# Turning the keys of a recurrent attention block: one whole-tile transpose and ScalarE copies in place of sixteen small transposes a unit

## The chip, the cores and the metric

The kernel runs on one core of a Trainium2 chip. A core has TensorE (PE, matmuls, with its weight loads shown apart as PEld), VectorE (DVE), ScalarE (ACT), GpSimd (POOL) and SyncE (SP, which issues transfers). Each engine works through its own instructions in the order in which they were written, and waits at semaphores for the others. The metric is the device time of one execution in microseconds; the median of three runs of the kernel before is 402.22 us.

## The reference

Two blocks follow each other. The first is a recurrent attention: with gates f = sigmoid(f_logit), a state of 48 x 48 for each of 4 batches and 8 heads is carried over 768 time steps.

```python
for t in range(S):
    state = f[:, :, t, :, None] * state + einsum('bhd,bhe->bhde', k[:, :, t], v[:, :, t])
    y[:, :, t] = einsum('bhd,bhde->bhe', q[:, :, t], state)
```

Its output, turned to 3072 tokens of 384 features, goes through the second block, a feed-forward layer with a maximum of three products:

```python
h = np.maximum(np.maximum(x @ w1, x @ w2), x @ w3)
return h @ w_out
```

## The kernel before, in words

**Units.** The attention is computed in 24 units (NU) of 64 time steps of two batches, so 128 tokens each. In a unit, features lie on the partitions: kh (the keys, scaled by the gates' products) and qh (the queries, scaled likewise) are 128 partitions by 512 elements: partition = one of two heads of a pair times 64 padded features; free = 4 head pairs, 2 batches, 64 tokens. The function scan (L342) makes running products of the gates on DVE; after turns the keys (L307, tile kt) and multiplies them to kh on POOL (L353); before does the same for the queries (L360, L307, L364).

**Keys by tokens.** The matmuls that add to the state (sums, L446) contract over tokens, so they need the keys with tokens on the partitions: ks, 128 tokens by 8 heads by 64. For units below 6 (BY_ROWS), PE turns them. For units 6 to 21, keys_by_blocks(u, n) does it for n = 0 to 3, one block of 32 tokens a call: four DVE transposes (L395) of 32 partitions by 128 elements, each of which turns 32 x 32 blocks of kh and writes them straight to the 32 partitions of the tokens.

**Order.** The order is written out by hand, and nothing reorders it. In a round of the loop over units u, with n = u + 1, five stretches of the second block's matmuls (fill) lie between the steps of the attention:

- a fill; keys_by_blocks(u, 2); values(u - 1), which writes the output bank y (L428) and ends with a 1x1 copy by ACT of one element of y (L435, tile seen); sums(u - 1) (L446); pairs(u) (L409, with the mask by DVE, L412); finish(u - 1), whose matmuls (L517) add to y and whose three ACT copies (L524) write xT; the new state (DVE, L461)
- loads; keys_by_blocks(u, 3); scan(n)
- a fill; after(n) and before(n); an ACT step of a check of the weights' range (L289)
- a fill; carry(n) (POOL, L370); a second ACT step of the check (L291)
- a fill; keys_by_blocks(n, 0)
- a fill; keys_by_blocks(n, 1); a third ACT step (L291); the sigmoids of unit u + 2 (ACT, L322, tile sig).

Between L435 and L517 there is a dependence: the last element that seen reads is one that L517 writes, so L517's first such matmul waits for ACT.

**The second block.** Groups of four units go through it with a lag of one group. Its matmuls are L555 and L802 for the first group and the preparation of the weights, L902 and L642 for the others. They write banks of PSUM that ACT and DVE read out in between: ACT by L910, L916, L925, L930, L937, L647, L698 and L727, DVE by L945, L952, L953 and L650. POOL makes sums of tiles (L606, L886) and adds (L920, L938). The order of their products and reads repeats with every four units from unit 9 on.

**Buffers.** The pool called work holds kh, ks and sig twice and kt (the turned keys of after) once.

Of the kernel before, what the change touches and what calls it, by code (L numbers as in the profile page):

```python
# [9 lines left out]
FP32 = mybir.dt.float32  # L10
# [36 lines left out]
C = 64  # L47
DP = 64
# [7 lines left out]
def kernel(  # L56
# [12 lines left out]
    nc = tc.nc  # L69
    B, H, S, D = q.shape  # L70
    HP = H // 2
    NU = B // 2 * (S // C)
    UT = 2 * C
# [16 lines left out]
    def fast():  # L90
        ctx = ExitStack()
        with ctx:
            work = ctx.enter_context(tc.tile_pool(name="work", bufs=2))
# [216 lines left out]
            ready = {}  # L310
# [74 lines left out]
            def keys_by_blocks(u, n):  # L385

                if BY_ROWS <= u < NU - 2:
                    kh = ready[u]["kh"]
                    if n == 0:
                        ready[u]["ks"] = work.tile([UT, H, DP], FP32, name="ks")  # L390
                    ks = ready[u]["ks"].rearrange("s (hp par) d -> s hp par d", par=2)
                    a, t0 = divmod(n * 32, C)
                    for p0 in range(0, 128, 32):
                        par, e0 = divmod(p0, DP)
                        nc.vector.transpose(ks[n * 32:(n + 1) * 32, :, par, e0:e0 + 32], kh[p0:p0 + 32, :, a, t0:t0 + 32])  # L395

            FOUR = [(par, a) for a in range(2) for par in range(2)]

# [620 lines left out]
            with tc.manual_schedule():  # L1019
# [123 lines left out]
                for step in HEAD.split():  # L1143
                    name = step.rstrip("0123456789")
# [4 lines left out]
                for u in range(GRP + 1, NU):  # L1149
                    n = u + 1  # L1150
                    part = EARLY if u < BY_ROWS else LATER if u < 2 * GRP else PART
                    if n == BY_ROWS:
                        scan(n)
                    fill(part)
                    keys_by_blocks(u, 2)
                    room_of_unit = room_of_pairs()
                    if u > GRP:
# [22 lines left out]
                    if u + 2 < NU:  # L1180
                        load_v(u + 2)
                    keys_by_blocks(u, 3)
                    if n < NU:
                        if n < BY_ROWS or n == BY_ROWS + 2:
# [26 lines left out]
                    if n == NU:  # L1211
                        finish(u, xT)
                        pack(3, 3, xT, both)
                        packed[u // GRP] = xT
                    keys_by_blocks(n, 0)
                    fill(part - 1000 if u < 2 * GRP else part)
                    keys_by_blocks(n, 1)
# [274 lines left out]
```

## Time and profile before

| | |
|---|---|
| median of three runs | 402.22 us (402.06 to 402.51) |
| span of the profiled execution, first to last instruction | 400.5 us |
| granted TensorE clock, mean | 0.998 |
| PE busy | 387.5 us |
| DVE busy | 297.6 us |
| POOL busy | 245.9 us |
| ACT busy | 179.8 us |

The profile is of one execution. The page gives the busy time of each engine, the span in slices, the chain of work that ended last, and the costliest groups of instructions by line. Other views show the instructions in order of time with the idle time of the engine before each and what released it, or sum up who waited for whom. L395 is line 395 of the kernel; an arrow such as ks<-kh names the tile written and the tile read. Times are in microseconds from the first instruction; the mean duration in a group is in nanoseconds.

### The profile page before, as it was taken

What the parts mean: (1) busy time and instruction counts of PE and PEld (TensorE: products, weight loads), DVE (VectorE), ACT (ScalarE), POOL (GpSimd) and SP (SyncE); (2) the same over time, 40 slices, a digit from 0 to 9 for tenths busy, and PEclk for the clock granted to TensorE, in tenths of its full rate; (3) what the DMA queues carried; (4) which work ended last, traced back from release to release, by engine and by line L of the source; (5) the groups of instructions that cost most, each with busy time, mean ns of one, the idle gap of its engine ahead of it and who ended that gap; (6) DMA issues with size and microseconds to landing.
All of it is one profiled execution on the core that took longest, in us unless ns stands there. A gap on an engine that the chain in (4) does not pass through costs nothing.

```text
span 400.5 us, 11665 instructions
## 1 busy us (share of the span) xinstructions
PE 387.5 (97%) x4654; PEld 338.4 (85%) x4654; DVE 297.6 (74%) x583; ACT 179.8 (45%) x430; POOL 245.9 (61%) x276
## 2 busy tenths in 40 slices
PE   5799999999999999999999999999999999999995
PEld 4678855569998889988899988899988899988995
DVE  7998998898989998987998997998985450012600
ACT  2588876413134523344532354434354335576110
POOL 2276655789997697287667377657577850525700
PEclk9999999999999999999999999999999999999999
DMA  8999877767564776776734577633672003541002
GB/s 166 249 286 303 227 194 119 151 99 124 104 92 89 117 132 151 124 121 87 153 90 84 75 117 94 172 53 72 85 160 82 1 19 102 133 142 61 2 20 64
DMA packets 181610, 47.21 MB, mean 118 GB/s; under 512 B 160496, under 2 KB 179248, under 8 KB 181552
## 3 DMA queue, kind: packets, MB, share of 16 engines
q1 hardware_dynamic: 177536, 45.52, 55.9%
q10 hardware_dynamic: 4016, 0.91, 1.1%
q8 instruction: 37, 0.61, 0.6%
q14 instruction: 21, 0.17, 0.1%
HBM read 37.75 MB, written 4.72 MB: 106 GB/s over the span
## 4 chain that ended last, share of the span: by engine, by line
PE 91%; DVE 4%; SPq 2%; issue 1%; DMA 1%; POOL 0%; DVEq 0%; POOLq 0%
PE p L902 20%; PE p L642 18%; PE tr L902 17%; PE tr L642 14%; PE p L555 6%; PE y L428 3%; PE p L802 3%; PE y L517 2%; PE a L409 2%; PE a L446 2%; SPq L187 2%; DVE r L342 1%; PE tr L302 1%; PE a L1086 1%; PE y L424 1%
## 5 line engine op out<-in xcount | busy, mean ns | idle before, releaser
L395 DVE STREAM_TRANSPOSE ks<-kh 32x128 f32<-32x128 f32 x256 | 77.4, 302 | 11.5 <-POOL kh L353 7.3
L902 PE MATMUL tr<-xT,placed 128*128 128x256 f32 x180 | 44.4, 384 | 0.0
L902 PEld LDWEIGHTS tr<-xT,placed 128*128 128x128 f32 x180 | 33.5, 190 | 4.9
L353 POOL TENSOR_TENSOR kh<-kt,r 128x512 f32<-128x512 f32 x18 | 31.9, 1772 | 8.5 <-DVE kt L307 8.5
L342 DVE TENSOR_TENSOR_SCAN r<-gate,from_one 128x520 f32<-128x520 f32 (+1 forms) x27 | 33.2, 1239 | 1.8 <-issue 1.2
L555 PE MATMUL p<-xT,w_in 128*128 128x256 f32 (+1 forms) x108 | 33.9, 456 | 0.0
L606 POOL TENSOR_TENSOR w_in<-hm 128x256 f32<-128x256 f32 x18 | 13.3, 738 | 32.5 <-DVE hm L953 29.8
L524 ACT COPY xT<-y 64x256 f32<-64x256 f32 (+1 forms) x60 | 22.1, 369 | 22.4 <-PE y L517 21.6
L269 POOL TENSOR_TENSOR w_in<-top_bits,rest_bits 128x384 uint32<-128x384 uint32 x18 | 21.0, 1170 | 16.4 <-DVE top_bits L262 12.2
L902 PE MATMUL tr<-xT,w_in 128*128 128x256 f32 x120 | 30.8, 379 | 0.0
L902 PE MATMUL p<-w_in,placed 128*128 128x256 f32 x120 | 30.4, 382 | 0.0
L650 DVE TENSOR_TENSOR o<-tr,w_in 128x384 f32<-128x384 f32 (+1 forms) x11 | 5.7, 521 | 33.0 <-PE tr L642 29.0
L642 PE MATMUL p<-placed,hm 128*128 128x192 f32 x144 | 29.7, 332 | 0.0
L902 PE MATMUL p<-xT,placed 128*128 128x256 f32 x120 | 29.2, 379 | 0.0
L642 PE MATMUL tr<-w_out,w_in 128*128 128x192 f32 x144 | 28.6, 326 | 0.0
L945 DVE TENSOR_TENSOR hm<-tr,hm 128x512 f32<-128x512 f32 x15 | 10.2, 683 | 22.8 <-PE tr L902 15.9
L352 POOL COPY ends<-r 128x8 f32<-128x8 f32 x18 | 5.7, 319 | 34.4 <-DVE r L342 34.4
L555 PEld LDWEIGHTS p<-xT,w_in 128*128 128x128 f32 x108 | 19.4, 190 | 8.4 <-issue 6.7
L902 PEld LDWEIGHTS p<-w_in,placed 128*128 128x128 f32 x120 | 22.4, 190 | 4.4 <-issue 1.5
L291 ACT ACTIVATE raw<-top_bits 128x384 f32<-128x384 f32 x48 | 25.2, 526 | 0.4
L902 PEld LDWEIGHTS tr<-xT,w_in 128*128 128x128 f32 x120 | 22.8, 190 | 3.1
L902 PEld LDWEIGHTS p<-xT,placed 128*128 128x128 f32 x120 | 22.7, 190 | 2.8
(183 smaller groups left out, 980.2 us busy)
## 6 DMA issues: line engine op xcount, KB each, us to landing
raw<-in_moe_w_dram SPq DMA_DIRECT2D x24, 384.0 KB, 4.4
v_ld<-in_v_dram SPq DMA_DIRECT2D x48, 96.0 KB, 3.5
placed<-in_moe_w_dram SPq DMA_DIRECT2D x12, 384.0 KB, 5.5
out_dram<-o SPq DMA_DIRECT2D x45, 96.0 KB, 2.2
placed<-in_moe_w_out_dram SPq DMA_DIRECT2D x6, 384.0 KB, 5.4
f_ld<-in_f_logit_dram SPq DMA_DIRECT2D x36, 64.0 KB, 2.9
k_ld<-in_k_dram SPq DMA_DIRECT2D x36, 64.0 KB, 2.6
q_ld<-in_q_dram SPq DMA_DIRECT2D x36, 64.0 KB, 2.5
```

What stands on the lines that cost most here:

```text
L269: nc.gpsimd.tensor_tensor(dst, by(top), by(rest), op=ALU.add)
L291: nc.scalar.activation(over, size, AF.Relu, scale=(-1 / HI_MIN, 1.0)[step - 1], bias=(1.0, -HI_END * (1 - 2.0 ** -24))[step - 1], accum_ou ...
L342: nc.vector.tensor_tensor_scan(r[:, x][:, ::-1], flat(gate)[:, x][:, ::-1], flat(from_one)[:, x][:, ::-1], 1.0, op0=ALU.mult, op1=ALU.max)
L353: (nc.vector if u < BY_ROWS else nc.gpsimd).tensor_tensor(kh.rearrange("p h a t -> p a h t"), kt, by_batch(r[:, 1:LEN + 1].rearrange("p (x ...
L395: nc.vector.transpose(ks[n * 32:(n + 1) * 32, :, par, e0:e0 + 32], kh[p0:p0 + 32, :, a, t0:t0 + 32])
L428: nc.tensor.matmul(y[o:o + DP, a, hp * C:(hp + 1) * C], lhsT=v_ld[s, 2 * hp + par, :], rhs=d["at"][s, par, hp, :], start=(hp == 0), stop=F ...
L524: nc.scalar.copy(xT[o, :, t0 + a * C:t0 + (a + 1) * C], y[i, a, 0:HP * C].rearrange("p (h t) -> p h t", h=HP))
L555: nc.tensor.matmul(p if w < TOK else p.rearrange("p (two t) -> p two t", two=2), lhsT=w_in[i][:, kt, j * 128:(j + 1) * 128], rhs=x[:, t.st ...
L606: engine.tensor_tensor(dst, x, y, op=op)
L642: nc.tensor.matmul(b[:, p * HD:(p + 1) * HD], lhsT=x, rhs=w, start=id(b) not in begun, stop=True, skip_group_check=True)
L802: nc.tensor.matmul(p[:, 0:DM], lhsT=w_in[0][:, a, j * 128:(j + 1) * 128], rhs=w_out[:, j, :], start=(j == 0), stop=(j == NJ - 1))
L902: nc.tensor.matmul(b[:, j * HALF:(j + 1) * HALF], lhsT=w[:, (2 * n + j) * 128:(2 * n + j + 1) * 128], rhs=x, start=begin and j == 0, stop= ...
```

## The change

At keys_by_blocks(u, 0), DVE now turns all of kh of the unit in one stream transpose, into a tile of 128 by 512 called turned. It takes its place in the single buffer of kt. A stream transpose turns each 32 x 32 block where it stands: the block of features e0 to e0 + 31 and tokens 32 n to 32 n + 31 ends up with its tokens on the partitions that the features had. In each of the four calls ACT then copies four such groups of blocks, 32 partitions by 4 x 32 elements, from the partitions p0 of their features to the partitions 32 n of their tokens in ks. Units below 6 and above 21 are as they were.

```diff
             def keys_by_blocks(u, n):
 
                 if BY_ROWS <= u < NU - 2:
-                    kh = ready[u]["kh"]
+                    d = ready[u]
                     if n == 0:
-                        ready[u]["ks"] = work.tile([UT, H, DP], FP32, name="ks")
-                    ks = ready[u]["ks"].rearrange("s (hp par) d -> s hp par d", par=2)
-                    a, t0 = divmod(n * 32, C)
+                        d["ks"] = work.tile([UT, H, DP], FP32, name="ks")
+                        d["turned"] = work.tile([128, 2 * HP, C], FP32, name="kt", bufs=1).rearrange(
+                            "p x t -> p (x t)").rearrange("p (h n d) -> p h n d", h=HP, d=32)
+                        nc.vector.transpose(d["turned"].rearrange("p h n d -> p h (n d)"),
+                                            d["kh"].rearrange("p h a t -> p h (a t)"))
+                    ks = d["ks"].rearrange("s (hp par) d -> s hp par d", par=2)
                     for p0 in range(0, 128, 32):
                         par, e0 = divmod(p0, DP)
-                        nc.vector.transpose(ks[n * 32:(n + 1) * 32, :, par, e0:e0 + 32], kh[p0:p0 + 32, :, a, t0:t0 + 32])
+                        nc.scalar.copy(ks[n * 32:(n + 1) * 32, :, par, e0:e0 + 32], d["turned"][p0:p0 + 32, :, n, :])
```

## The prediction

> **What bounds the kernel now.** First the page's busy times and the shares of its chain of waits, then busy time by stretch (columns: stretch, its length, busy time and instruction count of PE, PEld, DVE, ACT, POOL; granted clock, DMA share, GB/s).
>
> ```profile
> PE 387.5 (97%) x4654; PEld 338.4 (85%) x4654; DVE 297.6 (74%) x583; ACT 179.8 (45%) x430; POOL 245.9 (61%) x276
> PE 91%; DVE 4%; SPq 2%; issue 1%; DMA 1%; POOL 0%; DVEq 0%; POOLq 0%
> 240.00:270.00 30.00, 30.00 (x384) 26.78 (x383) 26.59 (x57) 12.57 (x30) 19.72 (x21) 1.00 0.57 106
> ```
>
> TensorE sets the end: in a stretch of the middle it is busy 30.00 of 30.00 us. DVE, busy 26.59 there, is nearly full but off the chain (4%). So no time is to be had by unloading DVE; the question is whether the added work on ACT stays hidden. ACT is busy only 12.57 of 30, but it serves its instructions in program order, and PE needs some of them at a fixed moment.
>
> **The prices.** The groups by line and form (count | busy us, mean ns | idle us before):
>
> ```profile
> L395 DVE STREAM_TRANSPOSE ks<-kh 32x128 f32<-32x128 f32 x256 | 77.4, 302 | 11.5 <-POOL kh L353 7.3
> L307 DVE STREAM_TRANSPOSE kt<-k_ld 128x512 f32<-128x512 f32 x18 | 12.3, 685 | 0.8 <-DMA q_ld<-in_q_dram 0.3 <-DMA f_ld<-in_f_logit_dram 0.3 <-DMA out_dram<-o 0.2
> L524 ACT COPY xT<-y 64x256 f32<-64x256 f32 x40 | 14.7, 367 | 0.6
> L245 ACT ACTIVATE top_bits<-top_bits 128x384 f32<-128x384 f32 x20 | 10.5, 524 | 0.6
> ```
>
> Removed: 256 DVE transposes of 302 ns, 16 for each of the units 6 to 21. Added on DVE: one whole-tile transpose a unit, priced like the keys' own, 0.69 us. DVE loses 77.4 - 16 x 0.69 = 66 us; worth nothing while PE is full. Added on ACT: 16 copies a unit of 32x128 floats. The trace has no ACT copy of this size from SBUF. Between L524's 367 ns for 256 elements and L698's 0.48 us for 384 (row below) ACT takes (480 - 367) / 128 = 0.88 ns an element. Going down from L245, which reads SBUF, 128 elements take 524 - 256 x 0.88 = 299 ns; going down from L524, which reads PSUM, 367 - 128 x 0.88 = 254 ns. The new copies read SBUF, so I take the first; three L524 copies in a row take 1.14 us (row below), some 0.02 each over their own time, hence 0.31 for a copy in a row of them, 1.24 for four, 79 us in all. Each group of four stands at the same four places of a unit, K0 to K3, where the four transposes stood.
>
> **Where they meet PE.** Each unit, ACT makes a 1x1 copy named seen (L435) of the output bank y; the matmuls of L517 write that place of y, so they cannot start before seen has read it, and PE's later matmuls queue behind them. K0 and K1 of unit n stand in the last part of the round before, K2 just ahead of the seen in unit n's own round. Timeline of unit 16 (start us, us, engine, line, tiles, count, idle before):
>
> ```profile
> 203.85 0.66 PE L409 MATMUL a<-qh,kh 48*64 48x64 f32 x32
> 204.07 1.25 DVE L395 STREAM_TRANSPOSE ks<-kh 32x128 f32<-32x128 f32 x4
> 205.34 0.69 DVE L412 TENSOR_TENSOR at<-a,mask 128x512 f32<-128x512 f32 x1
> 206.51 1.26 DVE L395 STREAM_TRANSPOSE ks<-kh 32x128 f32<-32x128 f32 x4
> ...
> 211.37 0.78 POOL L606 TENSOR_TENSOR w_in<-hm 128x256 f32<-128x256 f32 x1 [4.50 <-DVE hm L953]
> 212.12 0.48 ACT L647 COPY w_in<-p 128x384 f32<-128x384 f32 x1 [4.71 <-PE p L642]
> 215.37 0.48 ACT L698 COPY top_bits<-tr 128x384 f32<-128x384 f32 x1 [2.77 <-PE tr L642]
> 215.68 1.35 POOL L353 TENSOR_TENSOR kh<-kt,r 128x512 f32<-128x512 f32 x1
> 215.74 0.53 ACT L291 ACTIVATE raw<-top_bits 128x384 f32<-128x384 f32 x1
> 216.26 0.62 ACT L322 ACTIVATE sig<-f_ld 128x512 f32<-128x512 f32 x1
> 217.07 1.24 DVE L395 STREAM_TRANSPOSE ks<-kh 32x128 f32<-32x128 f32 x4 [1.07 <-POOL kh L353]
> 217.97 0.48 ACT L647 COPY w_in<-p 128x384 f32<-128x384 f32 x1 [1.09 <-PE p L642]
> 218.62 0.15 ACT L435 COPY seen<-y 1x1 f32<-1x1 f32 x1 [0.18 <-PE y L428]
> 219.31 0.63 PE L517 MATMUL y<-qh,state 48*48 48x64 f32 x32
> 220.00 1.14 ACT L524 COPY xT<-y 128x256 f32<-128x256 f32 x3 [1.23 <-PE y L517]
> ```
>
> Today DVE starts K0 at 217.07, as POOL's kh is ready only then; ACT has long gone on to L698 (215.37) and L291. In the changed kernel K0's copies stand on ACT between the first L647 and L698, and wait for the whole-tile transpose, which waits for kh. Behind that wait are queued L698, both steps of L291, sig, the second L647, K1, K2 and seen. Kh itself comes earlier: DVE drops the groups at 204.07 and 206.51. L412 still needs PE's pairs (end 204.51), so it gains 0.8 instead of 1.25, and with 1.26 the chain over DVE hm L953 to POOL's L606 and kh gains 2.0: the transpose runs 215.07 to 215.76. Bounds: 0 earlier (217.07) and 2.5 (214.57). Then ACT in order, waits of semaphores under 0.1 us left out: K0 to 217.00, L698 0.48 to 217.48, K1 to 218.72, L291 0.52 (to the next start) to 219.24, sig 0.62 to 219.86, L647 0.48 to 220.34, K2 to 221.58, seen 0.15 to 221.73. L517 starts there instead of at 219.31: PE stands 2.4 us. (L698 and L647 free banks that PE takes again only behind L517, so their lateness is in this stall already.) The stages repeat every four units, so units 12, 16 and 20 pay it: 7.2 us.
>
> Unit 18, two phases on:
>
> ```profile
> 241.30 1.24 DVE L395 STREAM_TRANSPOSE ks<-kh 32x128 f32<-32x128 f32 x4 [0.41 <-POOL kh L353]
> 243.73 0.59 ACT L925 COPY top<-tr 128x512 f32<-128x512 f32 x1 [1.95 <-PE tr L902]
> 244.59 0.59 ACT L930 COPY hm<-p 128x512 f32<-128x512 f32 x1 [0.28 <-PE p L902]
> 245.59 0.62 ACT L322 ACTIVATE sig<-f_ld 128x512 f32<-128x512 f32 x1
> 246.97 0.15 ACT L435 COPY seen<-y 1x1 f32<-1x1 f32 x1 [0.76 <-PE y L428]
> 247.66 0.63 PE L517 MATMUL y<-qh,state 48*48 48x64 f32 x32
> ```
>
> Here the transpose is done by 241.30 + 0.69 = 241.99 and K0 fits into the 1.95 us before L925. K1 stands behind L930, K2 behind sig; ACT has no gap from L930 to sig's end at 246.21. So seen ends at 246.21 + 2.48 + 0.15 = 248.84, against L517's 247.66: 1.2 us, for units 10, 14 and 18: 3.6 us.
>
> Unit 8, in the first round, has no L291 but little room:
>
> ```profile
> 97.42 0.63 ACT L322 ACTIVATE sig<-f_ld 128x512 f32<-128x512 f32 x1
> 98.94 0.48 ACT L698 COPY top_bits<-tr 128x384 f32<-128x384 f32 x1 [0.89 <-PE tr L642]
> 99.30 3.77 DVE L395 STREAM_TRANSPOSE ks<-kh 32x128 f32<-32x128 f32 x12
> 100.62 0.15 ACT L435 COPY seen<-y 1x1 f32<-1x1 f32 x1 [1.21 <-PE y L428]
> 101.25 0.63 PE L517 MATMUL y<-qh,state 48*48 48x64 f32 x32
> ```
>
> Transpose to 99.99, K0 and K1 to 102.47, sig to 103.10, L698 to 103.58, K2 to 104.82, seen to 104.97: 3.7 us behind 101.25. Unit 6 is alike; the last row is of the chain in order of time:
>
> ```profile
> 70.80 0.57 ACT L244 ACTIVATE top_bits<-placed 128x384 f32<-128x384 f32 x1
> 72.10 1.23 DVE L395 STREAM_TRANSPOSE ks<-kh 32x128 f32<-32x128 f32 x4
> 72.28 0.63 ACT L322 ACTIVATE sig<-f_ld 128x512 f32<-128x512 f32 x1
> 75.84 0.15 ACT L435 COPY seen<-y 1x1 f32<-1x1 f32 x1 [2.93 <-PE y L428]
> 76.70 0.45 PE y L517 x32
> ```
>
> K0 stands ahead of L244 and waits for the transpose's end, 72.79; ACT's work from 70.80 to sig's end, 72.91, is 2.1 us, all behind it: 72.79 + 2.1 + 3.72 + 0.15 = 78.76, 2.1 us late.
>
> In the odd units ACT's waits are long enough, as before unit 15's seen:
>
> ```profile
> 202.16 0.59 ACT L937 COPY top_bits<-p 128x512 f32<-128x512 f32 x1 [2.74 <-DVE hm L953]
> 203.64 0.15 ACT L435 COPY seen<-y 1x1 f32<-1x1 f32 x1 [0.90 <-PE y L428]
> ```
>
> K0 and K1 (2.48) go into 2.74 us of idle, K2 overruns 0.90 by 0.34, and between seen's end and L517 lay 0.54 in unit 16 (218.77 to 219.31). So nothing there. K3 stands behind L524, 220.00 + 1.14 + 1.24 = 222.4 in unit 16; its readers are the next unit's matmuls and, as the turned tile shares the one buffer of kt, the next L307; both are most of a unit away. If that cover is gone, DVE waits, not PE.
>
> **Sum:** 7.2 + 3.6 + 3.7 + 2.1 = 16.6 us on a span of 400.5. The runs' median, 402.2, lies 1.7 over the span and moves alike: 402.2 + 16.6, 419 us.
>
> [...] Whether copies overlap matters: L524's three of 367 ns or a little more take 1.14 us, so they follow one another without overlap, and I count the copies so. L291 though starts at 215.74, before L698's end at 215.85. [...]
>
> **Rivals.** (1) The copies overlap like L698 and L291, 0.1 us each: 0.21 for a copy, 0.84 for four. Unit 16's seen comes 1.2 earlier (stall 1.2), unit 18's 0.8 earlier (0.4), units 8 and 6 keep 2.5 and 0.9: 3.6 + 1.2 + 2.5 + 0.9 = 8.2, so 410. [...]
> (2) Kh comes no earlier, since POOL shares its time with other work: the stalls of 12, 16, 20 grow by 2.0 each, 425. For it: POOL's L606 to kh run without a gap; against: they wait 4.50 for DVE.
> (3) Not slower: seen is never late. In unit 16, from 215.76 to 219.31 there are 3.55 us; L698, L291, sig, L647 and seen take 2.25 and leave 1.30 for twelve copies, 0.11 each. Below that point the time stays at 402, and since PE has no idle to return, 0.5 us faster at best. For it: ACT is 55% idle; against: even the 1x1 copy takes 0.15.
>
> **Chances.** Forecast (415 to 423) 0.63; overlap 0.15; late kh 0.15; not slower 0.05; the rest, 0.02, slower still. A copy of 0.27 instead of 0.31 (the PSUM price with the gap) takes off 0.5 us where twelve copies count (units 6, 8, 12, 16, 20) and 0.3 where eight do, 3.4 in all; a transpose that gains 1 instead of 2 adds 3. The range takes in (1) and (2): 408 to 425. About 0.2% is what a measurement tells from no change: faster 0.02, same 0.03, slower 0.95.
>
> **What would show it.** Right: PE waits for ACT's seen before L517, 2 to 4 us in units 6, 8, 12, 16, 20, about 1 in 10, 14, 18, none in odd ones; ACT copies of about 0.31 us; DVE down 66 us and PE's busy time unchanged. Wrong: copies spaced 0.21 or less, the transpose of unit 16 no earlier against its L428, or PE waits at other evictions of ACT.

## The result, and the profile after

| | before | after |
|---|---|---|
| median, us | 402.37 (402.06 to 402.68, 4 runs) | 422.97 (421.11 to 425.47, 4 runs) |
| ratio to before, 95% interval | | 1.051 (1.046 to 1.056) |
| span of the profiled execution, us | 400.5 | 419.4 (its run: 421.11) |

The changed kernel is slower, by 20.6 us in the median and 18.9 us in the profiled executions. From the changed function on, its lines have numbers three higher than before: L517 is now L520, seen is L438, L647 is L650, L930 is L933.

From the page after: the busy times, the shares of its chain of waits and the costliest group; then, from the groups by line and form, the whole-tile transpose (columns as before):

```profile
PE 392.9 (94%) x4654; PEld 343.3 (82%) x4654; DVE 228.6 (54%) x343; ACT 255.2 (61%) x686; POOL 247.8 (59%) x276
...
PE 69%; ACT 13%; DVE 6%; POOL 4%; DMA 3%; SPq 3%; issue 2%; ACTq 0%; DVEq 0%; POOLq 0%
...
L398 ACT COPY ks<-kt 32x128 f32<-32x128 f32 x256 | 75.6, 295 | 21.6 <-DVE kt L393 18.6
```

```profile
L393 DVE STREAM_TRANSPOSE kt<-kh 128x512 f32<-128x512 f32 x16 | 11.3, 709 | 8.1 <-POOL kh L353 8.1
```

DVE gave up 69 us, ACT took 75.4, and ACT, with no share worth a line in the chain of before, now has 13% of it. PE stands idle for 26.5 us (419.4 - 392.9) instead of 13.0, and is busy 5.4 us longer with the same 4654 matmuls; 13.5 and 5.4 make the 18.9. The waits of PE after (who waited for whom: us in total, times, longest):

```profile
PE y L520 <- ACT seen L438: 14.2, 8, 2.5
...
PE p L905 <- ACT hm L933: 0.6, 3, 0.2
```

Eight waits at L520 for seen make 14.2 us, three at a readout 0.6; before, PE had no wait at either place. (PE's other waits, all in the first 80 us, shrank by some 1.2 us, so idle time grew by less than 14.8.) Unit 16 in order of time, first its values and L517 in the kernel before:

```profile
217.86 0.69 PE L428 MATMUL y<-at,v_ld 64*64 64x64 f32 x32
...
219.31 0.63 PE L517 MATMUL y<-qh,state 48*48 48x64 f32 x32
```

Then the same unit after:

```profile
226.01 0.71 DVE L393 STREAM_TRANSPOSE kt<-kh 128x512 f32<-128x512 f32 x1 [1.23 <-POOL kh L353]
...
226.76 1.22 ACT L398 COPY ks<-kt 32x128 f32<-32x128 f32 x4 [3.18 <-DVE kt L393]
...
227.89 0.46 ACT L701 COPY top_bits<-tr 128x384 f32<-128x384 f32 x1
...
228.36 1.22 ACT L398 COPY ks<-kt 32x128 f32<-32x128 f32 x4
...
228.84 0.69 PE L431 MATMUL y<-at,v_ld 64*64 64x64 f32 x32
...
229.60 0.52 ACT L291 ACTIVATE raw<-top_bits 128x384 f32<-128x384 f32 x1
...
230.12 0.61 ACT L322 ACTIVATE sig<-f_ld 128x512 f32<-128x512 f32 x1
...
230.64 0.46 ACT L650 COPY w_in<-p 128x384 f32<-128x384 f32 x1
231.11 1.21 ACT L398 COPY ks<-kt 32x128 f32<-32x128 f32 x4
...
232.34 0.15 ACT L438 COPY seen<-y 1x1 f32<-1x1 f32 x1
...
232.55 0.66 PE L520 MATMUL y<-qh,state 48*48 48x64 f32 x32 [2.08 <-ACT seen L438]
```

ACT stands 3.18 us for the transpose and then works without a gap, K0, L701, K1, both steps of L291, sig, L650, K2, to seen; L520 starts right behind it, 2.08 us after PE was free.

Most of PE's longer busy time is the clock. The granted clock by stretch, all engines (PE, PEld, DVE, ACT, POOL) for the first row, PE alone for the second; the number behind the busy times is the granted share:

```profile
166.00:174.00 8.00, 5.71 (x64) 5.49 (x56) 5.63 (x8) 5.16 (x17) 1.81 (x2) 0.79 0.13 27
```

```profile
234.00:242.00 8.00, 8.00 (x40) 0.79 0.50 73
```

Right behind the waits of units 12 and 16 the granted clock is 0.79 over 8 us, which is half the clock for 3.4 us: 8 x 0.21 = 1.7 us lost each time, 3.4 in this run. Another 1.4 of the 5.4 us is an overlap that is gone: L517 of unit 16 used to start 0.18 us before the end of the matmuls ahead of it (219.31, against L409's 218.83 + 0.66), and behind a wait it cannot, eight times. The last 0.6 us are not placed. The mean clock of the four runs is 0.990, 0.979, 0.982 and 0.987 for 421.11, 425.47, 423.69 and 422.25 us: the longer the run, the lower its clock. By these means the fastest run lost 0.010 x 419.4 = 4.2 us to it and the slowest 0.021 x 423.6 = 8.9, and the runs differ by 4.4.

### The profile page after: what moved, and what is told of

It is laid out like the page before. It is cut to its first block, busy times and chain, and to the rows that moved or that the text cites. A ratio compares the mean times of both kernels' runs of the same rounds, so it can differ in the third digit from the quotient of the medians.

```text
span 419.4 us, 11674 instructions
## 1 busy us (share of the span) xinstructions
PE 392.9 (94%) x4654; PEld 343.3 (82%) x4654; DVE 228.6 (54%) x343; ACT 255.2 (61%) x686; POOL 247.8 (59%) x276
## 4 chain that ended last, share of the span: by engine, by line
PE 69%; ACT 13%; DVE 6%; POOL 4%; DMA 3%; SPq 3%; issue 2%; ACTq 0%; DVEq 0%; POOLq 0%
PE p L905 16%; PE tr L905 13%; PE p L645 13%; PE tr L645 8%; PE p L558 6%; ACT ks L398 6%; SPq L187 2%; PE y L520 2%; POOL w_in L609 2%; PE y L431 2%; PE p L805 1%; DMA f_ld<-in_f_logit_dram 1%; DVE r L342 1%; PE a L412 1%; POOL hm L609 1%
## 5 line engine op out<-in xcount | busy, mean ns | idle before, releaser
L398 ACT COPY ks<-kt 32x128 f32<-32x128 f32 x256 | 75.6, 295 | 21.6 <-DVE kt L393 18.6
L923 POOL TENSOR_TENSOR hm<-hm,rest_bits 128x512 f32<-128x512 f32 x15 | 19.1, 1272 | 26.8 <-ACT hm L913 26.8
L353 POOL TENSOR_TENSOR kh<-kt,r 128x512 f32<-128x512 f32 x18 | 27.5, 1526 | 11.6 <-DVE kt L307 11.6
L342 DVE TENSOR_TENSOR_SCAN r<-gate,from_one 128x520 f32<-128x520 f32 (+1 forms) x27 | 32.1, 1198 | 2.1 <-issue 1.2
L645 PE MATMUL p<-placed,hm 128*128 128x192 f32 x144 | 32.3, 354 | 0.0
L415 DVE TENSOR_TENSOR at<-a,mask 128x512 f32<-128x512 f32 x19 | 13.1, 691 | 34.2 <-PE a L412 34.2
L645 PEld LDWEIGHTS p<-placed,hm 128*128 128x128 f32 x144 | 26.4, 207 | 1.4 <-ACT w_in L650 1.1
L650 ACT COPY w_in<-p 128x384 f32<-128x384 f32 x15 | 7.1, 474 | 33.4 <-PE p L645 33.4
```

The source lines that it names most:

```text
L342: nc.vector.tensor_tensor_scan(r[:, x][:, ::-1], flat(gate)[:, x][:, ::-1], flat(from_one)[:, x][:, ::-1], 1.0, op0=ALU.mult, op1=ALU.max)
L353: (nc.vector if u < BY_ROWS else nc.gpsimd).tensor_tensor(kh.rearrange("p h a t -> p a h t"), kt, by_batch(r[:, 1:LEN + 1].rearrange("p (x ...
L398: nc.scalar.copy(ks[n * 32:(n + 1) * 32, :, par, e0:e0 + 32], d["turned"][p0:p0 + 32, :, n, :])
L415: nc.vector.tensor_tensor(at, p[:, :, 0:HP * C].rearrange("s par (h t) -> s par h t", h=HP), mask.unsqueeze(1).unsqueeze(1).to_broadcast([ ...
L645: nc.tensor.matmul(b[:, p * HD:(p + 1) * HD], lhsT=x, rhs=w, start=id(b) not in begun, stop=True, skip_group_check=True)
L923: nc.gpsimd.tensor_tensor(out(n, 0), out(n, 0), first, op=ALU.add)
```

## The experiments

The theory under test, called the order theory in the expectations: PE loses time where an ACT instruction that it needs stands close behind a group of copies in ACT's order; at first I took that to be seen alone. The rivals: ACT's mere load of 75 us more, the buffer shared with kt, and the new transpose or its wait for kh.

**seen by VectorE.** The copies stay, the fence moves to another engine.

```diff
-                    nc.scalar.copy(seen, y[0:1, 1, (HP - 1) * C:(HP - 1) * C + 1])
+                    nc.vector.tensor_copy(seen, y[0:1, 1, (HP - 1) * C:(HP - 1) * C + 1])
```

> The changed kernel, but the 1x1 copy named seen is made by VectorE instead of ScalarE; all copies of the keys stay where they are. Order theory (L517's matmuls, now L520, wait for seen, which stands behind K0, K1 and K2 on ScalarE): the eight waits of PE at L520, 14.2 us, go. What is left are readouts by ScalarE that come late behind the copies, up to 1.2 us each in units 12, 16 and 20: 403 to 409 us, with a granted clock of 0.998. Load theory (75 us more on ScalarE delay whatever reads out PSUM): 420 us or more, since ScalarE has the same work.

Measured: 410.72 us against 401.62, ratio 1.023 (1.018 to 1.029). PE's waits:

```profile
PE p L645 <- ACT w_in L650: 2.0, 4, 0.8
PE tr L645 <- ACT w_in L809: 1.8, 1, 1.8
PE y L520 <- DVE seen L438: 1.3, 1, 1.3
...
PE p L905 <- ACT hm L933: 0.6, 3, 0.2
```

The 14.2 us at L520 are gone but for one wait for DVE, and more than half of the loss with them: 9.1 us are left of 20.6. The load theory, 420, falls. The time is 2 us over my range, and a part of the loss reappears at readouts by ACT that also stand behind copies (L650, L809). Taking seen away altogether was not tried, so no run shows whether the matmuls of values and finish, which write one place of y, need it.

**The same edit in the kernel before**, as a control.

> The kernel before, with seen made by VectorE: a control for the kernel after with the same edit. VectorE is busy 27 of 30 us there and its order has the transposes K2 ahead of seen, so PE may wait for it: if VectorE's queue is as far behind as its read of o was in unit 16 (218.34 against PE's L428 at 217.86), a wait of 0 to 2.5 us a unit in units 8, 12, 16, 20, 402 to 412 us in all. Load theory says nothing.

Measured: 418.33 us, ratio 1.041 (1.037 to 1.045). PE's waits, first row:

```profile
PE y L517 <- DVE seen L435: 13.3, 16, 1.4
```

So the fence costs on whichever engine's queue is behind: with the old transposes DVE's is, in sixteen waits over units of every phase, where I had thought of four units; the time is 6 us over the 402 to 412 expected. With DVE emptied by the change, one such wait was left.

**K2 behind seen.**

```diff
                     fill(part)
-                    keys_by_blocks(u, 2)
                     room_of_unit = room_of_pairs()
...
                         load_v(u + 2)
+                    keys_by_blocks(u, 2)
                     keys_by_blocks(u, 3)
```

> The changed kernel, with the four copies K2 moved behind seen and L527, next to K3. Order theory: each wait at L520 loses the 1.22 us of four copies: 2.30, 2.50, 0.68, 2.30, 1.19, 2.08, 1.19 and 1.96 become 1.08, 1.28, 0, 1.08, 0, 0.86, 0 and 0.74, in all 5.0 instead of 14.2, and if it takes a wait of about 2 us to halve the clock for 3.4 us, no such stretch is left: 408 us. Load theory: 421 us, as the sum of ScalarE's work is the same.

Measured: 417.08 us, ratio 1.037 (1.032 to 1.043). PE's waits:

```profile
PE y L520 <- ACT seen L438: 6.0, 5, 2.2
...
PE tr L905 <- ACT hm L913: 2.2, 4, 0.5
PE p L905 <- ACT hm L933: 1.5, 3, 0.5
...
PE p L645 <- ACT w_in L650: 1.3, 3, 0.5
PE tr L645 <- ACT w_in L809: 0.7, 1, 0.7
```

The waits at L520 fell to 6.0 in five places, near the 5.0 expected in five. But the four copies that were moved now stand ahead of other readouts (L913, L933, L650, L809), which cost 5.7 us. The time is 9 us over my number: a fence on seen alone is too narrow a theory. The load theory's 421 is not met either; this run by itself does not part the two.

**All copies behind seen.** The transposed tile has its own buffer, for which sig keeps one of its two (not in the lines below); the copies stand in four places of their unit's own round.

```diff
-                    keys_by_blocks(u, 2)
...
-                    keys_by_blocks(u, 3)
+                    copies(u, 0)
...
                     check_range(u - CHECKS, 0)
+                    copies(u, 1)
...
                     check_range(u - CHECKS, 1)
+                    copies(u, 2)
...
+                    copies(u, 3)
                     keys_by_blocks(n, 0)
                     fill(part - 1000 if u < 2 * GRP else part)
-                    keys_by_blocks(n, 1)
```

> The whole-tile transpose stays at K0, into a buffer of its own (sig has one buffer instead of two to make room), but all sixteen copies stand behind seen and L527 of their unit's own round: four where K3 was, four behind the step of L289, four behind the step of L291, four just ahead of the next unit's transpose. Order theory: no wait at L520, 402 to 404 us, with 75 us of copies on ScalarE as before. Load theory: 418 us or more.

Measured: 410.42 us, ratio 1.022 (1.020 to 1.024). No wait at L520 is left, as expected, but 402 to 404 is missed. Two rows of PE's waits, then ACT and PE in order of time around one of them (all lines four higher again: L933 is L937):

```profile
PE p L909 <- ACT hm L937: 4.4, 3, 1.5
...
PE p L649 <- ACT w_in L654: 2.2, 3, 0.7
```

```profile
240.69 1.22 ACT L402 COPY ks<-kturn 32x128 f32<-32x128 f32 x4
241.94 0.59 ACT L937 COPY hm<-p 128x512 f32<-128x512 f32 x1
...
242.67 1.10 PE L909 MATMUL p<-w_in,placed 128*128 128x256 f32 x4 [1.48 <-ACT hm L937]
```

L937 reads out a bank that PE takes again at once, and it is four copies late. The two rows make 6.6 of the 7.6 us by which this profiled execution is longer than that of the kernel before (408.1 against 400.5). The theory, mended: every readout that PE waits for counts, and for each the work in front of it on ACT.

**Copies in ACT's idle stretches.** With that theory I went through ACT's order for the seven kinds of round (units 6, 7 and 8, and the four places in a group) and chose, for each unit by its place in the group of four, places with idle time and no such readout close behind. All 256 copies stay on ACT.

```diff
...
+            PLACES = {0: (3, 5, 5, 5), 1: (1, 1, 5, 5), 2: (3, 4, 5, 6), 3: (3, 4, 5, 6)}
+            FIRST = {6: (3, 4, 5, 6), 7: (2, 4, 5, 5), 8: (3, 4, 5, 6)}
+            def copies_at(u, place):
+                for n, at in enumerate(FIRST.get(u, PLACES[u % GRP])):
+                    if at == place:
+                        copies(u, n)
...
```

(Place 1 stands where keys_by_blocks(n, 1) was, 2 where keys_by_blocks(u, 2) was, 3 where keys_by_blocks(u, 3) was, 4 behind before(n), 5 ahead of the second step of the check, 6 ahead of the next transpose.)

> As the kernel with all copies behind seen (own buffer for the turned tile), but each group of four copies stands in one of seven places of the two rounds, chosen by the unit's place in its group of four so that ScalarE has an idle stretch there and no readout that PE waits for comes close behind: for units of 4m, one behind L527 and three ahead of the second step of the range check; of 4m + 1, two with the sigmoids of the round before and two ahead of that step; of 4m + 2 and 4m + 3, one each behind L527, behind the queries, ahead of that step and ahead of the next transpose. Order theory, now for every readout and not for seen alone: 402 to 404 us with 256 copies on ScalarE. Load theory: 409 us or more, since ScalarE's work is that of the other kernel.

Measured: 401.57 us (10 runs) against 401.62, ratio 1.0008 (0.998 to 1.004): no difference. The page's busy times, the one wait for seen (its lines are 12 higher than after), and the group of copies:

```profile
PE 387.0 (97%) x4654; PEld 338.4 (85%) x4654; DVE 230.0 (58%) x343; ACT 254.3 (64%) x686; POOL 251.5 (63%) x276
```

```profile
PE y L532 <- ACT seen L450: 0.3, 1, 0.3
```

```profile
L402 ACT COPY ks<-kturn 32x128 f32<-32x128 f32 x256 | 75.7, 296 | 5.0 <-DVE kturn L393 1.4
```

With the same copies of the same price on ACT (254.3 us busy), and the same transpose on DVE, the loss is gone, and so is PE's longer busy time (387.0). That is the sharpest run: neither load nor the transpose costs anything here, the order does. Its buffers are those of the run own_buffer below, 424.32 us, so between these two only the places of the copies differ. It does not beat the kernel before, since PE was full there.

**The copies' place without their wait.** The kernel before, with its transposes, and 256 copies of a constant into a tile that nobody reads.

```diff
+            unused = keep.tile([UT, HP, 32], FP32, name="unused")
...
+                        nc.scalar.copy(unused[n * 32:(n + 1) * 32], causal[p0:p0 + 32].rearrange("p (h d) -> p h d", d=32))
```

> The kernel before, with its VectorE transposes, and beside them 256 ScalarE copies of 32x128 in the places of the change that read a constant and write a tile that nobody reads: the copies' cost without their wait for the transpose and for kh. Order theory: PE waits at L517 shrink to about 1.2, 1.2, 0.8, 0.8, 1.3, 0.8, 1.3, 0.8 in units 6, 8, 10, 12, 14, 16, 18, 20 plus 0.4 at three readouts: 9 us, 411 us. If the copies' place alone makes the loss, 417 to 421 us; if the wait for the transpose alone makes it, 402 to 404 us.

Measured: 412.09 us, ratio 1.027 (1.023 to 1.030). PE's waits (lines two higher than before):

```profile
PE y L519 <- ACT seen L437: 7.3, 8, 1.3
...
PE p L904 <- ACT hm L932: 0.8, 3, 0.3
```

Near the 411 expected: copies that wait for nothing make 7.3 us at that place, against 14.2, and the longest wait is 1.3 instead of 2.5. The other half I put down to ACT's wait for the transpose and kh, which pushes everything behind it, as the 3.18 us of unit 16 show; by subtraction only, since this run also keeps DVE's old transposes.

**A buffer of its own for the turned tile.**

```diff
-                    sig = work.tile([128, C // 32, 2 * HP, 32], FP32, name="sig")
+                    sig = work.tile([128, C // 32, 2 * HP, 32], FP32, name="sig", bufs=1)
...
-                        d["turned"] = work.tile([128, 2 * HP, C], FP32, name="kt", bufs=1).rearrange(
+                        d["turned"] = work.tile([128, 2 * HP, C], FP32, name="kturn", bufs=1).rearrange(
```

> The changed kernel, with a buffer of its own for the turned tile, so that the next keys need not wait for the four copies K3 (11.6 us of VectorE's waits; sig has one buffer instead of two to make room). Order theory: VectorE's wait there goes, and the time stays at 420 to 423 us. Buffer theory: 409 to 412 us.

Measured: 424.32 us, ratio 1.057 (1.051 to 1.063). PE's waits hardly differ from those after:

```profile
PE y L520 <- ACT seen L438: 14.4, 8, 2.5
```

The shared buffer costs DVE waits (11.6 us after at L307 for K3's copies, none here) and no time. The buffer theory falls. The same edit took one of sig's two buffers; nothing in PE's waits shows a gain that this could have hidden.

**The copies on VectorE.**

```diff
-                        nc.scalar.copy(ks[n * 32:(n + 1) * 32, :, par, e0:e0 + 32], d["turned"][p0:p0 + 32, :, n, :])
+                        nc.vector.tensor_copy(ks[n * 32:(n + 1) * 32, :, par, e0:e0 + 32], d["turned"][p0:p0 + 32, :, n, :])
```

> The changed kernel, with the sixteen copies of a unit on VectorE instead of ScalarE, in the same places. Both theories expect 402 to 403 us, since ScalarE is as in the kernel before; if the whole-tile transpose itself or its wait for kh cost PE time, the time stays well above. It also prices a VectorE copy of 32x128 from SBUF to SBUF: about 0.2 us would give VectorE 229 + 256 x 0.2 = 280 us busy.

Measured: 444.10 us, ratio 1.105 (1.100 to 1.110), against an expected 402 to 403. The view of the copies' line (shortest, median, longest duration in ns), the group, and a stretch of DVE and POOL:

```profile
L398 DVE COPY ks<-kt x256: 214/223/1883, 72.2 to 337.6; 32x128 f32<-32x128 f32 x128
```

```profile
L398 DVE COPY ks<-kt 32x128 f32<-32x128 f32 x256 | 123.8, 483 | 4.5
```

```profile
227.51 3.62 DVE L398 COPY ks<-kt 32x128 f32<-32x128 f32 x4
227.76 1.28 POOL L941 TENSOR_TENSOR top_bits<-top_bits,top 128x512 f32<-128x512 f32 x1
228.99 1.28 POOL L923 TENSOR_TENSOR hm<-hm,rest_bits 128x512 f32<-128x512 f32 x1
230.22 0.84 POOL L370 TENSOR_TENSOR state<-st,ends 128x384 f32<-128x384 f32 x1
```

My price of 0.2 us holds for the median (223 ns) and not for the sum: 115 of the 256 copies take over 0.3 us, 92.7 us together, and each of these ends 74 to 85 ns after the end of a POOL instruction. Four copies beside POOL's work take 3.62 us here. So on DVE this copy is dearer (483 ns) than the transpose it replaces (302 ns), and DVE is 349 us busy. PE's two largest groups of waits:

```profile
PE y L520 <- ACT seen L438: 10.9, 4, 3.5
PE a L412 <- POOL qh L364: 7.3, 3, 4.9
```

Seen is late here with no copy of the keys on ACT: for the longest of these waits ACT stood 7.93 us for DVE's hm (L956) to make its readout L940, and seen comes behind that. A wait in the fence's queue does what work in it does. The run does not tell whether the whole-tile transpose is free; the one with the copies in idle stretches does.

## Why the prediction was right, point by point

419 us (408 to 425) was forecast, 422.97 measured.

- **The mechanism** was right: L517 (L520) waits for seen behind K0, K1 and K2, in the eight units named. No odd unit waits there, as forecast. Two signs came out otherwise: PE's busy time, forecast unchanged, grew by 5.4 us, and PE waits at another readout of ACT too, L933, though for 0.6 us in all.
- **The copy's price:** 0.31 us with its gap, 1.24 for four; measured 295 ns and 1.22. **The transpose:** 0.69 us, measured 0.71. DVE's 66 us less were 69.
- **Kh earlier by 2.0 us:** forecast 2.79 us ahead of unit 16's values (215.07 against 217.86), measured 2.83 (226.01 against 228.84). The rival of the late kh was wrong.
- **K3's cover** was thought to be most of a unit; DVE waited for K3's copies eight times, 11.6 us, and PE not at all, as the prediction had it for that case.
- **The stalls:** 16.6 us forecast. The forecast counts from L517's start in the kernel before, the rows of waits from the end of PE's work before it, 0.18 later; so their 14.2 us are not the same thing. From the values to L517 (L520) it was 1.45 us in unit 16 before (217.86 to 219.31) and 3.71 after (228.84 to 232.55): 2.26, where 2.4 was forecast. Counted so, the eight units make 15.6 us. Unit 6, 2.1 forecast, makes 2.5 (its wait, 2.30, is the first row below); unit 8, for which I had 3.7, makes 2.7. That term failed by its start: I left unit 8's transpose at 99.30, 0.5 ahead of the values at 99.81, and it starts 1.6 ahead now. DVE had dropped the transposes of unit 7, but that is not the gain: it then stood 2.35 us for sig, late behind copies on ACT, and turned the gates 7.0 us ahead of the values, 7.2 before. What is gone is a wait of 0.57 us of the queries' transpose for three of POOL's sums, which took 3.97 us before and 2.10 after; why they are shorter stays open. PE of unit 6, then DVE and PE of unit 8, after:

```profile
78.55 0.67 PE L520 MATMUL y<-qh,state 48*48 48x64 f32 x32 [2.30 <-ACT seen L438]
```

```profile
100.16 0.71 DVE L393 STREAM_TRANSPOSE kt<-kh 128x512 f32<-128x512 f32 x1
...
101.74 0.70 PE L431 MATMUL y<-at,v_ld 64*64 64x64 f32 x32
```

- **Overlap or not:** I counted the copies by L524's row, without overlap, and that was right. Four copies in 1.22 us are 0.31 us from start to start, at 295 ns each. The rival that took the 0.1 us of the pair L698 and L291 for the copies, 410, fell. That the new copies move rows to other partitions does not account for it: L701 starts at 227.89, before the end of K0's last copy (226.76 + 1.22 = 227.98), and that copy moves rows; and four of a unit's sixteen copies stay on their partitions, yet the copies of a group start 11 to 13 ns after the end of the one before alike. Why they do not overlap stays open.
- **What the sum lacked:** the clock. Every term was a wait, and none the slower matmuls behind a wait: 3.4 us in the profiled run, more in runs of a lower mean clock. So the prediction came close with two errors of opposite sign, 1.0 us too much of waits (16.6 against 15.6) and 3.4 us or more of clock left out; the first is unit 8's, since the smaller misses of the other seven cancel. That waits and clock offset each other in part is luck.

## What to carry to other kernels

Work that is moved to an engine with idle time is only free where it stands: walk that engine's order, and for each instruction that the bounding engine waits for, add up what stands between it and the last wait, the new waits included. A busy share of 45% said nothing here; the same 256 copies cost 20 us in one order and nothing in another. A 1x1 copy that only serves as a fence deserves the same look as a large readout.

## What the runs showed of the hardware that I had not expected

- Two of PE's waits of about 2 us were followed by a stretch at half the granted clock. In the profiled run after, the clock is 0.50 from 169.05 to 172.46 us and from 233.90 to 237.31, 3.41 us each, and 1.00 in the 61.44 us between them. The first stretch begins 0.60 us after the end of unit 12's wait of 2.29 us, the second 1.35 us after the end of unit 16's of 2.08. Behind the waits of 2.30 and 2.50 us in units 6 and 8 there is none (1.00 from 75 to 82 us and from 102 to 112), nor behind the 1.96 of unit 20 (1.00 from 290 to 310). What sets the two kinds of waits apart is not shown. The mean clock of the runs was 0.979 to 0.990 after and 0.977 to 0.986 with the buffer of its own, where the longest wait for seen is 2.5 us, and 0.994 to 1.000 with the unused copies, where it is 1.3, much as in the kernel before (0.993 to 1.000).
- The 256 VectorE copies of 32x128 in the run with the copies on VectorE took 214 to 1883 ns, 223 in the median. All 115 that took over 0.3 us end 74 to 85 ns behind the end of a POOL instruction. The stream transposes of the same shape in the kernel before took 302 ns on the mean and at most 308, with or without work of POOL beside them: 146 of the 256 lie wholly within an instruction of POOL and took 302 ns on the mean, and the 41 that touch none took 304. Why the copies were longer there and the transposes were not stays open.
